# Bank order of the P·V runs, engine of the weight-scale operations, and room for side work in a fused attention and GLU kernel

## The chip, the cores and the metric

The kernel runs on one core of a Trainium2 chip. The metric is the device time of one execution in microseconds (us). Three executions of the kernel before took 2601.76, 2604.6 and 2605.78 us; their median is 2604.6 us. The five engines of a core, with the short names that the profile uses, are TensorE (PE, its weight loads PEld), VectorE (DVE), ScalarE (ACT), GpSimd (POOL) and SyncE (SP, which only issues transfers).

## The reference

The input `x` has 2048 rows of 576 numbers. Everything is computed in float32:

```python
xn = layernorm(x)                         # over the 576 columns
qkv = xn @ wqkv                           # 32 heads of 18 columns each
p = softmax(q @ k.T * 18 ** -0.5)         # 2048 x 2048 for each head
s = (p @ v, heads side by side) @ wo
h = gelu(xn @ w_gate) * (xn @ w_up)       # 2048 x 4608, tanh form of gelu
g = silu(h @ w_down)
out = x + s * g
```

## The kernel before

**Precision.** Most products are taken in float16 with each float32 operand split in a high and a low half (`XHT`, `XL` for the normalized input, `whi`, `wlo` for weights, `hhi`, `hlo` for the hidden values), three products for one. To split a weight block, its largest magnitude is found, and the block is scaled by a power of two.

**Preparing a weight block.** `prep` makes a list of small steps ("pieces") for each block: load by DMA, seven maxima on VectorE (`amax`, `amaxd`, lines 248 and 253), a trip through DRAM that spreads the maximum over the partitions (`par`, `spread`), then on VectorE `top` (line 295), `power` (line 300: the bits of the exponent are kept), `floor` (line 306), `inverse` (a reciprocal, line 311, and a multiplication, line 312), then the splits (`split_hi` on ScalarE, line 330, and `split_lo` mostly on GpSimd, lines 337 and 338), and for the 18 gate/up/down blocks `units` and `back` (lines 316 to 324), which give the factors by which results are scaled back. From `power` on these are eight small operations, each on 128 partitions by one or two numbers. Where a block is `urgent` (the first two) some of this goes another way. There are 25 such blocks: the first attention block, V, four more attention blocks, 18 gate/up/down blocks and the output projection.

**The order of work is written out by the program.** Each engine executes its instructions in the order in which they are issued here. The main loop goes over 16 pairs of heads, `p`, with 64 steps `i` each; `now` is 64 `p` + `i`. A step issues the scores for the softmax (`qk2`, line 1337, into the PSUM bank `s2`, then the exponential on ScalarE, line 1343), the scores for the row maxima of a later pair (`qk1`, line 1285, into `s1`, then the maximum on VectorE, line 1288), and beside these one share of the other products: slots of a gate/up product or a projection (`Pair`, line 468, called "g" in the code), a stage of a down product (`DownPair`, line 728, bank `md`), or a run of P times V.

**Gate/up pairs.** A `Pair` writes two PSUM banks, `ma` (gate) and `mb` (up). When its last slot is issued, `end` puts an evacuation of the gate bank on ScalarE at once (line 633); one step later the up bank follows (line 644), and one more step later four elementwise operations on GpSimd (`cubic`, lines 656 to 659). Later come a tanh on ScalarE (line 662), two operations on GpSimd (669, 670), and the split of the result (684, 691).

**Runs of P times V.** The exponentials wait in `pend`, two half steps to a unit. When a `Pair` has closed (`gs.closed`), the next step issues a run: `flush` takes the units out of `pend` in bursts, each burst into the next bank of the tuple that it is given, and cuts a burst where one block of queries ends (the unit whose third entry is `NT - 1`) and the next begins. `burst` (line 1362) adds its bank to `osum` on VectorE (line 1370) or, for the first burst of a query block, copies it (line 1368). With a down stage in the same step the banks are `ma`, `mb`; without one they are `md`, `ma`. The `Pair` that comes after the run begins with `ma`.

**Side work.** `subtick(room, most)` is called once a step. It first gives out deferred operations that are due (`Deferred.advance`), then at most `most` pieces of the weight preparation, first in, first out. `room` says how many microseconds of ScalarE ("A") and VectorE ("V") work may be given out; a piece with the cost `None` always fits. A `Rest` holds the list until so much planned time has gone by, a `Gate` until a condition holds. In the step of a run `room["V"]` is 2.2, or 1.4 if a down product ends in it (`late`); in other steps it is 0.75 or 0.25.

Of the kernel before, what the change touches and what calls it, by code (L numbers as in the profile page):

```python
# [12 lines left out]
F32 = mybir.dt.float32  # L13
F16 = mybir.dt.float16
I32 = mybir.dt.int32
# [5 lines left out]
P = 128  # L21
# [64 lines left out]
def on_dve(t=0.7):  # L86
    return {"V": t}
# [7 lines left out]
def kernel(ctx: ExitStack, tc: tile.TileContext, x, wqkv, wo, w_gate, w_up, w_down, out):  # L95
# [55 lines left out]
    def subtick(room=FREE, most=3):  # L151
        defer.advance(room)
        n = 0
        while bg and n < most:
            if isinstance(bg[0], Gate):
                if not bg[0].open():
                    return
                bg.popleft()
                continue
            if isinstance(bg[0], Rest):  # L160
                if not bg[0].over():
                    return
                bg.popleft()
                continue
            cost, fn = bg[0]
            if not defer.fits(cost):
                return
            defer.spend(cost)
            bg.popleft()
            n += 1  # L170
            if fn is None:
                return
            fn()
# [36 lines left out]
    def prep(name, parts, n, down=None, urgent=False, free=None, dfree=None, lead=1, vec=()):  # L210
# [80 lines left out]
        def top():  # L291
            k = w.k
            if not urgent:
                w.mg = sm.tile([P, 2], F32, tag="mg", name=f"mg_{name}")
                nc.vector.tensor_reduce(w.mg[:, 0:k], w.mb.rearrange("p a k -> p k a"), op=ALU.max, axis=AX.X)

        def power():
            k = w.k
            w.E = sm.tile([P, 2], F32, tag="E", name=f"E_{name}", bufs=4)
            nc.vector.tensor_scalar(  # L300
                w.E[:, 0:k].bitcast(I32), w.mg[:, 0:k].bitcast(I32), 0x7F800000, None, op0=ALU.bitwise_and
            )

        def floor():
            k = w.k
            nc.vector.tensor_scalar(w.E[:, 0:k], w.E[:, 0:k], 2.0 ** -60, None, op0=ALU.max)

        def inverse():
            k = w.k
            w.s = sm.tile([P, 2], F32, tag="s", name=f"s_{name}")  # L310
            nc.vector.reciprocal(w.s[:, 0:k], w.E[:, 0:k])
            nc.vector.tensor_scalar(w.s[:, 0:k], w.s[:, 0:k], 2.0 ** 14, None, op0=ALU.mult)

        def units():
            w.uE = sm.tile([P, 2], F32, tag="uE", name=f"uE_{name}", bufs=4)
            nc.vector.tensor_scalar(w.uE[:, 0:1], w.E[:, 0:1], 2.0 ** -24, None, op0=ALU.mult)
            nc.vector.tensor_scalar(w.uE[:, 1:2], w.s[:, 0:1], 2.0 ** -44, None, op0=ALU.mult)

        def back():
            w.c = sm.tile([P, 1], F32, tag="c", name=f"c_{name}", bufs=4)  # L320
            nc.vector.tensor_scalar(
                w.c, w.E[:, 0:1], w.E[:, 0:1], 2.0 ** -9, op0=ALU.mult, op1=ALU.mult
            )
            nc.vector.tensor_tensor(w.c, w.c, w.E[:, 1:2], op=ALU.mult)

        def split_hi(t):
            if t == 0:
# [30 lines left out]
        def add(fn, cost=None):  # L358
            pieces.append((cost, fn))

        def rest(span):
            if not urgent:
                pieces.append(Rest(span))
# [16 lines left out]
        rest(6.5)  # L380
        add(top, on_dve(0.4))
        for fn in (power, floor, inverse):
            add(fn, on_dve(0.2))
        rest(0.5)
        if free is not None:
            pieces.append(Gate(free))
        for t in range(5):
# [2 lines left out]
                add(lambda t=t: split_lo(t - 1), low_cost[t - 1])  # L390
        add(lambda: split_lo(4), low_cost[4])
        if down is not None:
            add(units, on_dve(0.2))
            add(back, on_dve(0.3))
            add(fin)
            pieces.append(Gate(dfree))
            add(lambda: dsplit_hi(0), act)
            add(lambda: dsplit_hi(1), act)
            add(lambda: dsplit_lo(0), on_pool(3.0))
            add(lambda: dsplit_lo(1), on_pool(3.0))  # L400
            add(dfin)
        else:
            add(fin)
# [1058 lines left out]
    k = 0  # L1462
# [113 lines left out]
    def flush(tags):  # L1576

        for tag in tags:
            if not pend:
                return  # L1580
            n = next((k + 1 for k, u in enumerate(pend) if u[2] == NT - 1), len(pend))
            burst(pend[:n], tag)
            del pend[:n]
# [36 lines left out]
    for p in range(NPAIR):  # L1620
# [3 lines left out]
        for i in range(4 * NT):  # L1624
# [64 lines left out]
            else:  # L1689
# [16 lines left out]
                if gs.closed:  # L1706
                    gs.closed = False
                    if late:
                        dn.evac()
                        dn = None  # L1710
                    subtick({"A": 2.2, "V": 1.4 if late else 2.2, "T": 0.7 + 0.86 * len(pend) + 0.73 * d}, 6)
                    flush(("ma", "mb") if d else ("md", "ma"))
                    summed = not d
                else:
                    quick = late or step is not None and step[2] < 1.45 and len(bg) < 70
                    subtick({
                        "A": 0.75, "V": 0.25 if quick else 0.75,
                        "T": 2.0 if step is None else 0.45 + step[2],
                    })
                    if late:  # L1720
                        dn.evac()
                        dn = None
                    g_run(7 if step is None else step[1] or 0)
                    if behind:
                        dn = DownPair()
                        dn.run()
# [73 lines left out]
```

## Time and profile before

| | |
|---|---|
| runs | 2601.76, 2604.6, 2605.78 us |
| profiled execution, its own time | 2606.5 us |
| its span, first to last instruction | 2604.7 us |
| mean granted TensorE clock | 0.995 |
| busy: VectorE | 1929.3 us (74%) |
| busy: ScalarE | 1660.6 us (64%) |
| busy: GpSimd | 1508.9 us (58%) |
| mean DMA traffic | 46 GB/s |

The first exponential of the main loop starts at 214.7 us; before it the input is normalized, V and the first heads are projected, and the first gate/up products begin. The profile's views that matter here are the page, the waits (who waited for whom, how long in total, how often, the longest), the timeline (start, duration, engine, line, what is written and read; in brackets the idle time of the engine before it and what ended it), and the groups of instructions by line. The rows themselves stand where the prediction uses them.

### The profile page before, as it was taken

What the parts mean: (1) busy time and instruction counts of PE and PEld (TensorE: products, weight loads), DVE (VectorE), ACT (ScalarE), POOL (GpSimd) and SP (SyncE); (2) the same over time, 40 slices, a digit from 0 to 9 for tenths busy, and PEclk for the clock granted to TensorE, in tenths of its full rate; (3) what the DMA queues carried; (4) which work ended last, traced back from release to release, by engine and by line L of the source; (5) the groups of instructions that cost most, each with busy time, mean ns of one, the idle gap of its engine ahead of it and who ended that gap; (6) DMA issues with size and microseconds to landing.
All of it is one profiled execution on the core that took longest, in us unless ns stands there. A gap on an engine that the chain in (4) does not pass through costs nothing.

```text
span 2604.7 us, 60777 instructions
## 1 busy us (share of the span) xinstructions
PE 2510.1 (96%) x25800; PEld 1326.4 (51%) x25800; DVE 1929.3 (74%) x2712; ACT 1660.6 (64%) x2081; POOL 1508.9 (58%) x1428
## 2 busy tenths in 40 slices
PE   6899999999999999999999999999999999999988
PEld 6564545455544545455554454555445444454555
DVE  7587778777877778777777777777777777677644
ACT  5225666666767666766666666767666665766664
POOL 4246663576537543757667575748566675757513
PEclk9999999999999999999999999999999999999999
DMA  4431021201130112111010110101111111010124
GB/s 143 124 107 24 12 58 57 60 18 44 39 84 19 27 37 64 39 30 51 14 50 13 38 45 21 49 15 38 29 33 29 37 29 40 17 38 8 41 62 137
DMA packets 134300, 118.68 MB, mean 46 GB/s; under 512 B 60176, under 2 KB 113064, under 8 KB 134028
## 3 DMA queue, kind: packets, MB, share of 16 engines
q1 hardware_dynamic: 128892, 105.23, 15.1%
q0 software_dynamic: 2432, 6.54, 0.8%
q8 instruction: 201, 3.29, 0.6%
q10 hardware_dynamic: 2704, 3.03, 0.4%
q14 instruction: 71, 0.58, 0.1%
HBM read 84.89 MB, written 29.61 MB: 44 GB/s over the span
## 4 chain that ended last, share of the span: by engine, by line
PE 81%; DVE 9%; ACT 4%; issue 2%; DMA 2%; POOL 2%; SPq 0%; ACTq 0%; DVEq 0%; POOLq 0%
PE mb_t L468 16%; PE ma_t L468 15%; PE md_t L728 15%; PE md_t L1362 9%; PE s L1337 8%; PE s L1285 8%; PE ma_t L1362 6%; DVE PM L1288 3%; ACT P L1343 1%; PE md_t L907 1%; DVE osb L1370 1%; DVE m_c L248 1%; PE mb_t L1362 1%; DMA QT<-QD 1%; PE mb_t L907 1%
## 5 line engine op out<-in xcount | busy, mean ns | idle before, releaser
L1288 DVE TENSOR_REDUCE PM<-s 128x2 f32<-128x1024 f32 x1024 | 1250.5, 1223 | 340.9 <-PE s L1285 332.6
L1343 ACT ACTIVATE P<-s,etab 128x1024 f32<-128x1024 f32 x896 | 995.7, 1112 | 615.7 <-PE s L1337 600.1
L468 PE MATMUL ma_t<-XHT,whi_c 64*128 64x512 f16 x1440 | 542.5, 377 | 10.5 <-DVE osb L1368 5.6
L468 PE MATMUL mb_t<-XHT,whi_c 64*128 64x512 f16 x1440 | 542.5, 377 | 3.8 <-DVE touch L436 2.0
L468 PE MATMUL ma_t<-XHT,wlo_c 64*128 64x512 f16 x1296 | 487.9, 376 | 0.0
L468 PE MATMUL mb_t<-XHT,wlo_c 64*128 64x512 f16 x1152 | 433.5, 376 | 0.0
L468 PE MATMUL ma_t<-XL,whi_c 64*128 64x512 f16 x1152 | 433.3, 376 | 0.0
L468 PE MATMUL mb_t<-XL,whi_c 64*128 64x512 f16 x1152 | 433.2, 376 | 0.0
L1285 PE MATMUL s<-KT,QT 54*128 54x512 f16 x2048 | 399.5, 378 | 20.8 <-DVE PM L1288 9.5
L1337 PE MATMUL s<-QT,KT 56*128 56x512 f16 x2048 | 406.2, 380 | 5.3 <-ACT P L1343 1.6
L468 PEld LDWEIGHTS <-whi_c 64*128 64x128 f16 x5184 | 276.7, 94 | 245.0 <-issue 29.5
L728 PE MATMUL md_t<-dhi_c,hhi 64*128 64x288 f16 x2304 | 341.8, 283 | 7.3 <-DVE osb L1370 2.3
L728 PE MATMUL md_t<-dhi_c,hlo 64*128 64x288 f16 x2304 | 341.5, 282 | 0.0
L728 PE MATMUL md_t<-dlo_c,hhi 64*128 64x288 f16 x2304 | 340.9, 282 | 0.0
L669 POOL TENSOR_SCALAR tw<-tw 128x512 f32<-128x512 f32 x144 | 90.9, 632 | 408.1 <-ACT tw L662 408.0
L728 PEld LDWEIGHTS <-hhi 64*128 64x128 f16 x4608 | 247.2, 94 | 141.3 <-issue 22.8
L1362 PE MATMUL md_t<-P,VT 128*32 128x512 f32 x2480 | 293.0, 596 | 0.7 <-ACT P L1343 0.5
L691 POOL TENSOR_TENSOR hlo<-gv,hhi 128x512 f16<-128x512 f32 x144 | 168.0, 1167 | 206.4 <-ACT hhi L684 195.8
L1337 PEld LDWEIGHTS <-KT 56*128 56x128 f16 x2048 | 126.0, 94 | 244.4 <-issue 158.0
L656 POOL TENSOR_TENSOR tw<-gs 128x512 f32<-128x512 f32 x144 | 150.6, 1046 | 138.8 <-ACT gs L633 138.3
L748 DVE SCALAR_TENSOR_TENSOR y<-md_t,c_c,y 128x576 f32<-128x576 f32 x272 | 219.0, 805 | 8.3 <-PE md_t L728 8.2
L468 PEld LDWEIGHTS <-wlo_c 64*128 64x128 f16 x2592 | 139.6, 94 | 121.8 <-issue 1.1
(253 smaller groups left out, 4070.3 us busy)
## 6 DMA issues: line engine op xcount, KB each, us to landing
draw_c<-in_B_w_down SPq DMA_DIRECT2D x18, 576.0 KB
raw_c<-in_B_w_gate SPq DMA_DIRECT2D x18, 512.0 KB
raw_c<-in_B_w_up SPq DMA_DIRECT2D x18, 512.0 KB
obr<-rd SPq DMA_DIRECT2D x30, 256.0 KB
KT<-KD SPq DMA_DIRECT2D x32, 224.0 KB
QT<-QD SPq DMA_DIRECT2D x32, 216.0 KB
VS<-vst POOLq DMA_DIRECT2D x16, 304.0 KB, 4.0
VT<-VS SPq DMA_DIRECT2D x16, 304.0 KB
```

What stands on the lines that cost most here:

```text
L468: nc.tensor.matmul(o, lw, xx, start=self.stage == 0 and self.k == 0, stop=self.stage == 1 and self.k == self.slots - 1, skip_group_check=True,
L656: gp.tensor_tensor(st["t"], st["g"], st["g"], op=ALU.mult)
L669: gp.tensor_scalar(st["t"], st["t"], 1.0, 1.0, op0=ALU.mult, op1=ALU.add)
L691: gp.tensor_tensor(hs.lo[:, ft], st["v"], hs.hi[:, ft], op=ALU.subtract)
L728: nc.tensor.matmul(self.t.t[:, hf, 0:288], a[r, ft, sl], b[r, ft, 288 * hf:288 * hf + 288], start=self.stage == 0 and k == 0, stop=self.st ...
L748: nc.vector.scalar_tensor_tensor(yy, y, w.c, yy, op0=ALU.mult, op1=ALU.add)
L907: nc.tensor.matmul(o, a, b, start=self.stage == 0 and self.k == 0, stop=self.stage == 1 and self.k == len(terms) - 1, skip_group_check=True,)
L1285: nc.tensor.matmul(s1[:, h], QT[p][r, P * qt:P * qt + P], KT[p][r, 512 * kb:512 * kb + 512], start=True, stop=True)
L1288: nc.vector.tensor_reduce(PM[p][:, :, qt, kb:kb + 1], s1, op=ALU.max, axis=AX.X)
L1337: nc.tensor.matmul(s2[:, h], KT[p][r, P * kt:P * kt + P], QT[p][r, 512 * qb:512 * qb + 512], start=True, stop=True)
L1343: nc.scalar.activation(pt, s2, AF.Exp, scale=ETAB[j0])
L1362: nc.tensor.matmul(t.t[qd:qd + 32, :], VT[p][:, c0:c0 + 32], pt[:, h], start=kt == k0, stop=kt == k1, skip_group_check=True,)
```

## The change

Three things are edited.

1. `flush` is given `("ma", "md")` instead of `("md", "ma")` where no down stage runs in the step and a query block ends inside the run, before its last unit (`two`).
2. For blocks that are not urgent, `floor`, `inverse`, `units` and `back` are issued to GpSimd (`small_ops`). `power` stays on VectorE and gets a second operation that makes the complement of the exponent in `w.s`; `inverse` is then one operation (minimum and multiplication) instead of a reciprocal and a multiplication. `back` becomes three operations instead of two. `floor` and `inverse` of these blocks, and `units` and `back` always, have no cost for the planner now. The pause after them is 1.0 instead of 0.5.
3. In the step of a run the room for VectorE is 0.8 instead of 1.4 if a down product ends in it; otherwise it stays 2.2 while `now` is under 256 (the first four pairs of heads) and is 1.5 instead of 2.2 from then on.

```diff
+        small_ops = nc.vector if urgent else nc.gpsimd
+        EXPO = 0x7F800000
+
         def power():
             k = w.k
             w.E = sm.tile([P, 2], F32, tag="E", name=f"E_{name}", bufs=4)
+            w.s = sm.tile([P, 2], F32, tag="s", name=f"s_{name}")
+            mg = w.mg[:, 0:k].bitcast(I32)
+            nc.vector.tensor_scalar(w.E[:, 0:k].bitcast(I32), mg, EXPO, None, op0=ALU.bitwise_and)
             nc.vector.tensor_scalar(
-                w.E[:, 0:k].bitcast(I32), w.mg[:, 0:k].bitcast(I32), 0x7F800000, None, op0=ALU.bitwise_and
+                w.s[:, 0:k].bitcast(I32), mg, EXPO, EXPO, op0=ALU.bitwise_and, op1=ALU.bitwise_xor
             )
 
         def floor():
             k = w.k
-            nc.vector.tensor_scalar(w.E[:, 0:k], w.E[:, 0:k], 2.0 ** -60, None, op0=ALU.max)
+            small_ops.tensor_scalar(w.E[:, 0:k], w.E[:, 0:k], 2.0 ** -60, None, op0=ALU.max)
 
         def inverse():
             k = w.k
-            w.s = sm.tile([P, 2], F32, tag="s", name=f"s_{name}")
-            nc.vector.reciprocal(w.s[:, 0:k], w.E[:, 0:k])
-            nc.vector.tensor_scalar(w.s[:, 0:k], w.s[:, 0:k], 2.0 ** 14, None, op0=ALU.mult)
+            small_ops.tensor_scalar(
+                w.s[:, 0:k], w.s[:, 0:k], 2.0 ** 61, 2.0 ** 13, op0=ALU.min, op1=ALU.mult
+            )
 
         def units():
             w.uE = sm.tile([P, 2], F32, tag="uE", name=f"uE_{name}", bufs=4)
-            nc.vector.tensor_scalar(w.uE[:, 0:1], w.E[:, 0:1], 2.0 ** -24, None, op0=ALU.mult)
-            nc.vector.tensor_scalar(w.uE[:, 1:2], w.s[:, 0:1], 2.0 ** -44, None, op0=ALU.mult)
+            small_ops.tensor_scalar(w.uE[:, 0:1], w.E[:, 0:1], 2.0 ** -24, None, op0=ALU.mult)
+            small_ops.tensor_scalar(w.uE[:, 1:2], w.s[:, 0:1], 2.0 ** -44, None, op0=ALU.mult)
 
         def back():
             w.c = sm.tile([P, 1], F32, tag="c", name=f"c_{name}", bufs=4)
-            nc.vector.tensor_scalar(
-                w.c, w.E[:, 0:1], w.E[:, 0:1], 2.0 ** -9, op0=ALU.mult, op1=ALU.mult
-            )
-            nc.vector.tensor_tensor(w.c, w.c, w.E[:, 1:2], op=ALU.mult)
+            small_ops.tensor_tensor(w.c, w.E[:, 0:1], w.E[:, 0:1], op=ALU.mult)
+            small_ops.tensor_scalar(w.c, w.c, 2.0 ** -9, None, op0=ALU.mult)
+            small_ops.tensor_tensor(w.c, w.c, w.E[:, 1:2], op=ALU.mult)
...
         add(top, on_dve(0.4))
         for fn in (power, floor, inverse):
-            add(fn, on_dve(0.2))
-        rest(0.5)
+            add(fn, on_dve(0.2) if urgent or fn is power else None)
+        rest(0.5 if urgent else 1.0)
...
         if down is not None:
-            add(units, on_dve(0.2))
-            add(back, on_dve(0.3))
+            add(units)
+            add(back)
             add(fin)
...
-                    subtick({"A": 2.2, "V": 1.4 if late else 2.2, "T": 0.7 + 0.86 * len(pend) + 0.73 * d}, 6)
-                    flush(("ma", "mb") if d else ("md", "ma"))
+                    subtick({"A": 2.2, "V": 0.8 if late else 2.2 if now < 256 else 1.5, "T": 0.7 + 0.86 * len(pend) + 0.73 * d}, 6)
+                    two = any(u[2] == NT - 1 for u in pend[:-1])
+                    flush(("ma", "mb") if d else ("ma", "md") if two else ("md", "ma"))
                     summed = not d
```

## The prediction

> **What bounds the kernel now.** I read the page first, then the busy times by stretch, then who waited for whom on PE in the main loop, 240 to 2400 us.
>
> ```profile
> span 2604.7 us, 60777 instructions
> PE 2510.1 (96%) x25800; PEld 1326.4 (51%) x25800; DVE 1929.3 (74%) x2712; ACT 1660.6 (64%) x2081; POOL 1508.9 (58%) x1428
> ...
> 240.00:2400.00 2160.00, 2122.59 (x21768) 1079.62 (x21762) 1655.13 (x2264) 1448.18 (x1790) 1335.07 (x1227) 1.00 0.14 36
> ...
> PE s L1285 <- DVE PM L1288: 7.9, 8, 2.1
> PE ma_t L468 <- DVE osb L1368: 5.6, 10, 2.3
> PE ma_t L468 <- DVE osb L1370: 3.9, 6, 1.1
> ```
>
> PE is the bound: 96% of the span, and in the main loop 2122.59 of 2160 us. The change removes no matmul, so its reach there is the 37.4 us in which PE idles, and most of that waits for DVE. The second line of waits is the one that the bank order aims at: ten times a gate/up pair wanted bank ma, and the copy out of it by line 1368 was not done. The other two are places where DVE came late after a run of P times V, with small side work ahead of it. The head and the tail (0 to 240, 2400 to the end) hold few of the steps that change: the two urgent blocks keep DVE and have four small operations up to the scale before and after. I cost them at nothing. A change within 0.2%, some 5.2 us, can't be told from none here; that is the meaning of "same" below.
>
> **Part A, the bank order.** One of the ten boundary runs, then a worse one, the other long one, and a run that begins with ma today because a down stage stands ahead of it:
>
> ```profile
> 1262.07 0.69 ACT L633 ACTIVATE gs<-ma_t,uE_c 128x512 f32<-128x512 f32 x1 [0.68 <-PE ma_t L468]
> 1262.33 1.07 PE L1362 MATMUL md_t<-P,VT 128*32 128x512 f32 x8
> 1262.81 0.13 PEld L1362 LDWEIGHTS ma_t<-P,VT 128*32 128x32 f32 x4 [0.32 <-ACT gs L633]
> 1263.59 0.68 DVE L1370 TENSOR_TENSOR osb<-md_t,osb 128x512 f32<-128x512 f32 x1
> 1264.32 0.69 DVE L1368 COPY osb<-ma_t 128x512 f32<-128x512 f32 x1
> 1265.07 0.37 PE L468 MATMUL ma_t<-XHT,whi_c 64*128 64x512 f16 x1 [0.27 <-DVE osb L1368]
> ...
> 746.18 0.68 DVE L1370 TENSOR_TENSOR osb<-md_t,osb 128x512 f32<-128x512 f32 x1
> 746.78 0.68 DVE L1368 COPY osb<-ma_t 128x512 f32<-128x512 f32 x1
> 747.51 0.56 PE L468 MATMUL ma_t<-XHT,whi_c 64*128 64x512 f16 x1 [2.35 <-DVE osb L1368]
> ...
> 1340.84 1.86 DVE L248 TENSOR_REDUCE m_c<-raw_c 128x1 f32<-128x512 f32 x3
> 1343.95 0.37 PE L468 MATMUL ma_t<-XHT,whi_c 64*128 64x512 f16 x1 [1.04 <-DVE osb L1368]
> ...
> 960.25 1.07 PE L1362 MATMUL ma_t<-P,VT 128*32 128x512 f32 x8 [0.48 <-ACT gs L633]
> ```
>
> What goes: eight of the ten waits are the plain kind, 0.27 us each (5.6 less 2.35 and 1.04, by eight). With ma first, its sum runs on DVE while PE works on the burst in md, so ma is free in time, and eight times 0.27 go, 2.2 us. At 747 us DVE itself was late (three maxima ahead); PE would be let go at the end of the sum instead of the end of the copy, 0.60 us earlier. At 1344 us one maximum fewer stands ahead (part C), and the whole 1.04 goes. The md copy is late next, but a down stage that follows such a run is put behind the gate/up slots by `behind`, so nobody asks for md at once.
>
> What comes: ma can't be written before ScalarE has read the gate out of it. In the first rows that evacuation runs from 1262.07 to 1262.76; the burst started at 1262.33 in md, and the weight load for ma was released at 1262.81, by the evacuation. With ma first the whole run starts at 1262.81, 0.48 us later, and PE has nothing in between. At 960 us just that wait is in the trace, 0.48 us, even with a down stage ahead of it. So each plain boundary loses 0.48 and gains 0.27: +0.21 by eight, +1.7. At 747 the burst's delay lies inside DVE's lateness, so it stays at -0.6; at 1344 it is 0.48 less 1.04, -0.6. **A: +0.5 us.** Its ends are -3.8 (the new wait is covered after all) and +4.2 (0.48 ten times less 0.6, were the DVE lateness not met again).
>
> **Part B, the small operations.** One late stretch, the worst of its kind, with the start of the gate evacuation:
>
> ```profile
> 2203.88 0.69 ACT L633 ACTIVATE gs<-ma_t,uE_c 128x512 f32<-128x512 f32 x1 [0.19 <-PE ma_t L468]
> ...
> 2207.04 1.27 POOL L658 TENSOR_TENSOR tw<-tw,gs 128x512 f32<-128x512 f32 x1
> 2207.07 1.27 DVE L306 TENSOR_SCALAR E_c<-E_c 128x2 f32<-128x2 f32 x1
> 2208.27 1.26 POOL L659 TENSOR_TENSOR gv<-gv,gs 128x512 f32<-128x512 f32 x1
> 2208.64 0.92 DVE L312 TENSOR_SCALAR s_c<-s_c 128x2 f32<-128x2 f32 x1
> 2211.33 0.39 PE L1285 MATMUL s<-KT,QT 54*128 54x512 f16 x2 [2.06 <-DVE PM L1288]
> ...
> L306 DVE TENSOR_SCALAR E_c<-E_c x18: 92/170/1282, 163.9 to 2207.1; 128x2 f32<-128x2 f32 x18
> ```
>
> `floor` works on two numbers a partition, takes 170 ns in the median and 1282 at most. At 2207 it lasts until GpSimd's operation ends (2208.34 against 2208.31), then the multiplication likewise (until 2209.56, against 2209.53). So a small DVE operation is held by a large one on GpSimd, and DVE's next work, the sum of the run and the row maximum, comes late: PE loses 2.06 us. The Trainium skill's page "SBUF — State Buffer", section "Who interferes with whom", has the rule: a DVE tensor_scalar in a two-port mode and a GpSimd operation take one pair of ports exclusively, for the whole instruction. The trace agrees (the two ends, 0.03 us apart).
>
> In the step of a run `top`, `power`, `floor`, `inverse` are all issued in the run's own subtick, while `cubic` is issued one step later. So the new GpSimd `floor` and `inverse` stand ahead of `cubic` in GpSimd's queue, and wait there for `power`: GpSimd is idle while DVE does its two bit operations, and these aren't held. Where, instead, `power` falls a step later, `cubic` is ahead, and both bit operations can be held, one after the other. PE's waits behind these chains:
>
> ```profile
> 439.91 0.39 PE L1285 MATMUL s<-KT,QT 54*128 54x512 f16 x2 [1.04 <-DVE PM L1288]
> ...
> 522.58 0.37 PE L468 MATMUL ma_t<-XHT,whi_c 64*128 64x512 f16 x1 [1.11 <-DVE osb L1370]
> ...
> 716.83 0.30 PE L728 MATMUL md_t<-dhi_c,hhi 64*128 64x288 f16 x2 [0.78 <-DVE osb L1370]
> ...
> 1503.67 1.22 DVE L300 TENSOR_SCALAR E_c<-mg_c 128x2 int32<-128x2 int32 x1
> 1504.83 1.26 POOL L659 TENSOR_TENSOR gv<-gv,gs 128x512 f32<-128x512 f32 x1
> 1505.00 0.30 PE L728 MATMUL md_t<-dhi_c,hhi 64*128 64x288 f16 x2 [1.00 <-DVE touch L436]
> ...
> 1611.08 0.37 PE L468 MATMUL ma_t<-XHT,whi_c 64*128 64x512 f16 x1 [1.01 <-DVE osb L1370]
> ```
>
> At 523, 1611 and 2211 us the chain was held in a run's step: 1.1 + 1.0 + 2.1 go. At 440 nothing was held; the reciprocal and the multiplication go, half a microsecond. At 717 it was `units` and `back` ahead of the sum: 0.8 goes. At 1505 the wait is that of a down stage in an ordinary step, so I take `power` there to be of the later kind: it stays held for 1.22, and the second bit operation comes as line 659 begins, so it is held for about another 1.2: +1.2. **B: -5.5 + 1.2 = -4.3 us.** Ends: -6.5 (at 1505 nothing is held either, and its 1.0 goes) and -2.0 (the second operation is held wherever `floor` was: 0.9 goes at 2211, the multiplication's hold, half a microsecond each at 440, 523 and 1611, 0.8 at 717, and 1505 costs its 1.2).
>
> GpSimd gets seven operations a gate/up block. The trace has no such one; by the nearest rows
>
> ```profile
> L1166 POOL TENSOR_TENSOR xn<-xt,xn 128x64 f16<-128x64 f32 x16 | 5.1, 320 | 33.2 <-ACT xn L1165 31.9 <-PE pv_t L415 1.3
> L1276 POOL MEMSET VT<- 128x16 f32 x16 | 1.8, 112 | 0.0
> ...
>   POOL tw L658: 3.0, 5
> ...
> 1165.52 1.27 POOL L658 TENSOR_TENSOR tw<-tw,gs 128x512 f32<-128x512 f32 x1
> ...
> 1170.98 0.62 ACT L662 ACTIVATE tw<-tw 128x512 f32<-128x512 f32 x1
> ```
>
> one lies between 112 ns (16 columns written) and 320 ns (64 columns read and written); I take 200, nearer to the memset because there are fewer columns still. 18 x 7 x 0.2 is 25 us of an engine that is idle for some 1100, so its time is covered. The added wait isn't free: behind `floor` in GpSimd's queue stands `cubic`, behind that the tanh on ScalarE, behind that exponentials, and PE. `cubic` can start now when the gate evacuation ends (2204.57 in the stretch above), some 2.3 us ahead of `power` (0.2 before `floor` at 2207.07), and would start about 0.8 us after `power` begins (two bit operations, `floor`, `inverse`, 0.2 each): up to 3.1 us later. The tanh in the last two rows, one case, begins 4.2 us after the GpSimd result that it needs, and ScalarE's idle time for it is 3.0 us over five waits in all. I put down +0.4 us, between nothing and 3 us.
>
> **Part C, less room beside a run.**
>
> ```profile
> L1343 ACT ACTIVATE P<-s,etab x896: 1095/1113/1127, 214.7 to 2575.3; 128x1024 f32<-128x1024 f32 x180
> ...
> 1038.34 0.39 PE L1285 MATMUL s<-KT,QT 54*128 54x512 f16 x2 [2.12 <-DVE PM L1288]
> ...
> 2178.68 0.30 PE L728 MATMUL md_t<-dhi_c,hhi 64*128 64x288 f16 x2 [0.83 <-DVE osb L1368]
> ```
>
> Sixteen pairs of heads take from 214.7 to 2575.3, 147.5 us each, so `now` is 256 near 805 us. From there a room of 1.5 lets two pieces at 0.7 through in place of three. Three maxima of 0.62 us (the row at 1340.84, 1.86 for three) stood ahead of DVE's sum at these two places; one fewer is -0.6 each. The piece that is pushed out goes to an ordinary step, where DVE has a quarter of its time free; I found no PE wait over 0.4 us behind a lone maximum of an ordinary step, so I cost that at nothing, with 3 us as its other end (five such waits of 0.6). **C: -1.2 us.**
>
> **The sum.** +0.5 - 4.3 + 0.4 - 1.2 = -4.6 us. The profiled execution took 2606.5 us, 1.8 beyond its span, and would come to 2601.9. The median of the runs is 1.9 below the profiled one, so the forecast for a median is 2604.6 - 4.6 = **2600.0 us**, 0.18% faster.
>
> **The rivals.** *Faster.* All small operations pass unheld, B at -6.5 with A and C as they are: 2604.6 + 0.5 - 6.5 - 1.2 = 2597.4; if the gate evacuation is covered as well (A at -3.8), 2593.1. For it: the hold needs GpSimd at work, and its queue now stops at `floor`. Against: the rows at 1262 and 960 us show the evacuation as the later of the two. *Nothing gained.* By the skill's rule the first to issue keeps the ports; should `cubic` mostly be ahead, the second bit operation takes the place of `floor`, B is -2.0, and the sum +0.5 - 2.0 + 0.4 - 1.2 = -2.3: 2602.3. For it: 1503.67. Against: the run began long before it there, and `cubic` is issued a step after the run's subtick. *Slower.* GpSimd, stopped at `floor` until a late DVE reaches `power`, passes its lateness to tanh, exponentials and PE. It decides from the point where `cubic` comes more than 4.2 us later than now; at 1 us beyond that in each of 18 blocks it costs 18 us less the 4.6: 2618. Against it: the 3.1 us above.
>
> **How the numbers follow.** The forecast's case has 0.50, with an own range of 2597 to 2604; its part under 2599.4 (0.2% faster) is about 0.14, the rest "same". Faster rival 0.28. Nothing gained 0.14, same. Slower rival 0.08. So faster 0.42, same 0.50, slower 0.08. The range, 2593.5 to 2605.5, takes in the faster rival but its outer end and the case of nothing gained, and leaves out the slower one.
>
> **What would show it.** Copies by line 1368 read md instead of ma at some ten places; PE's wait for them at ma is gone, and a new wait, ma at line 1362 for the gate evacuation, has about 4 us in ten waits where 1.8 in two stood. Lines 306, 312 and 316 to 324 stand on POOL; the bit operations at line 300 and the next take 170 ns, except where they meet `cubic`. The waits of line 1285 for line 1288 fall from 7.9 to some 4. Waits of the tanh for line 658 of over 6 us in all would speak for the slower rival; no new wait at line 1362 would show part A wrong, and a PE total below 2509 or above 2512 would show that the matmuls themselves changed.

## The result and the profile after

The changed kernel takes 2589.04 us (median of six runs, 2588.17 to 2589.88) against 2604.98 us before (2601.76 to 2606.47). The ratio is 0.994, with a 95% interval from 0.9929 to 0.9951: 16 us or 0.6% faster, clear of noise, beyond the low end of the forecast's range (2593.5) and more than three times the 4.6 us that were forecast. The page of the changed kernel (its span, then busy time and share of each engine):

```profile
span 2588.1 us, 60831 instructions
PE 2503.7 (97%) x25800; PEld 1317.9 (51%) x25800; DVE 1898.9 (73%) x2594; ACT 1661.0 (64%) x2081; POOL 1537.7 (59%) x1564
```

Read this beside the page of before. The matmuls are the same 25800, VectorE does 118 operations fewer, GpSimd 136 more. The span is 16.6 us shorter, but PE's busy time, which no step of the prediction touched, fell by 6.4 us of that. The waits of PE between 240 and 2400 us (who, on whom, us in total, times, longest):

```profile
PE ma_t L1367 <- ACT gs L638: 4.7, 10, 1.0
PE s L1290 <- DVE PM L1293: 4.6, 7, 1.5
PE s L1342 <- ACT P L1348: 4.0, 5, 1.6
PE ma_t L473 <- DVE osb L1375: 2.6, 5, 1.0
```

The first line is new in this size (1.8 in two waits before): runs that begin with ma wait for the gate evacuation. The waits for line 1368 (now 1373) at ma are gone, 5.6 us before. The row maxima fell from 7.9 to 4.6. The third line is new too: two waits of 1.6 us for exponentials.

Both kernels issue the same matmuls in the same order, apart from bank names and 14 of the 25800 that change places with a neighbour. So their starts can be matched one by one, and every change of the distance between two starts belongs to one place. Those that the argument uses, worked out from the two traces:

```
matmul at (before, after), us   change there   what it waited for before / after
 439.91   438.51    -0.60   row maximum, behind the small operations / the same, shorter
 522.58   519.31    -1.28   sum, behind held small operations / nothing
 523.18   519.32    -0.59   the copy after it / nothing
 716.83   711.84    -0.99   sum, behind units and back / nothing
 741.84   737.82    +0.97   nothing / evacuation of ma (bank order)
 747.51   741.93    -1.57   copy out of ma / sum out of ma (bank order)
1038.34  1029.84    -0.66   row maximum, three maxima ahead / the same, shorter
1262.33  1254.60    +0.47   nothing / gate evacuation (bank order; seven more like it)
1265.07  1256.90    -0.43   copy out of ma / nothing     (bank order; seven more like it)
1343.95  1334.49    -1.20   copy out of ma, three maxima ahead / nothing
1505.00  1494.43    -1.16   down stage, behind a held power / nothing
1547.04  1538.23    +1.78   nothing / exponential
1551.96  1542.37    -0.79   sum of a run / the same, shorter
1611.08  1600.10    -1.17   sum, behind held small operations / nothing
1866.48  1853.55    -0.79   down stage, behind a held floor / nothing
1906.05  1894.93    +1.79   nothing / exponential
2178.68  2165.81    -1.00   copy, three maxima ahead / nothing
2211.33  2195.81    -2.22   row maximum, behind held small operations / nothing
```

Two things are to be seen. A plain boundary wait shows 0.27 us idle in the brackets, but costs 0.43 from start to start: the idle time counts only from the modelled end of the last matmul, which lasts 0.38 us where the next could start after 0.21. Some 0.16 us of each wait therefore stands under "busy". And some waits go on costing after they end. The timeline of the kernel before, PE's rows around the worst boundary wait (start, duration):

```profile
747.51 0.56 PE L468 MATMUL ma_t<-XHT,whi_c 64*128 64x512 f16 x1 [2.35 <-DVE osb L1368]
...
747.87 0.63 PE L468 MATMUL ma_t<-XL,whi_c 64*128 64x512 f16 x1
...
748.29 0.63 PE L468 MATMUL ma_t<-XHT,wlo_c 64*128 64x512 f16 x1
```

and its windows view over that stretch and the next (length, PE busy and matmuls, granted clock, DMA share, GB/s):

```profile
747.50:751.10 3.60, 3.59 (x18) 0.53 0.27 78
751.10:754.70 3.60, 3.59 (x34) 1.00 0.13 36
```

The matmuls run in pairs, one for ma and one for mb (left out here). After the wait, the pairs start 0.42 us apart instead of 0.21, and a matmul lasts 0.63 instead of 0.38. The granted clock is 0.53 for 3.6 us, and 18 matmuls pass in place of 34: some 1.7 us beyond the wait. The same follows the wait at 2211 us. Both are gone in the changed kernel's profiled run. The two stretches at half speed make up some 3.1 us of the 6.4 us that PE's "busy" time lost. The rest lies in the hidden parts of waits and in small steps, which were not counted one by one.

### The profile page after: what moved, and what is told of

Read it like the earlier page. It is cut to its first block, busy times and chain, and to the rows that moved or that the text cites. A ratio compares the mean times of both kernels' runs of the same rounds, so it can differ in the third digit from the quotient of the medians.

```text
span 2588.1 us, 60831 instructions
## 1 busy us (share of the span) xinstructions
PE 2503.7 (97%) x25800; PEld 1317.9 (51%) x25800; DVE 1898.9 (73%) x2594; ACT 1661.0 (64%) x2081; POOL 1537.7 (59%) x1564
## 4 chain that ended last, share of the span: by engine, by line
PE 83%; DVE 6%; ACT 4%; POOL 3%; issue 2%; DMA 1%; ACTq 0%; SPq 0%; DVEq 0%; POOLq 0%
PE mb_t L473 16%; PE ma_t L473 15%; PE md_t L733 15%; PE md_t L1367 10%; PE s L1342 8%; PE s L1290 8%; PE ma_t L1367 6%; DVE PM L1293 2%; ACT P L1348 1%; PE md_t L912 1%; DVE osb L1375 1%; PE mb_t L1367 1%; PE mc_t L492 1%; PE mb_t L912 1%; PE pv_t L492 1%
```

## The experiments

Each kernel was timed against the kernel before on the same chip, in five rounds. That kernel's medians there were 2604.25 to 2605.73 us, so a difference of 1 to 2 us between two rows of the table shows nothing by itself.

| kernel | median, us | ratio to before, 95% interval |
|---|---|---|
| changed kernel | 2589.04 | 0.9940 (0.9929 to 0.9951) |
| `a_banks`: bank order alone | 2603.75 | 0.9996 (0.9987 to 1.0005) |
| `b_small`: small operations alone | 2596.97 | 0.9972 (0.9962 to 0.9983) |
| `c_room`: smaller room alone | 2597.36 | 0.9972 (0.9963 to 0.9981) |
| `a_and_b` | 2596.14 | 0.9967 (0.9954 to 0.9979) |
| `b_and_c` | 2590.45 | 0.9950 (0.9936 to 0.9964) |
| `columns` | 2596.41 | 0.9969 (0.9958 to 0.9981) |
| `columns_room` | 2596.83 | 0.9971 (0.9961 to 0.9982) |
| `units_room` | 2599.26 | 0.9982 (0.9973 to 0.9990) |
| `units_dve` | 2589.27 | 0.9941 (0.9928 to 0.9955) |
| `units_early` | 2588.17 | 0.9941 (0.9929 to 0.9954) |
| `halves` | 2602.72 | 0.9994 (0.9985 to 1.0003) |
| `columns_room_halves` | 2607.09 | 1.0009 (1.0000 to 1.0018) |
| `shift_a` | 2615.22 | 1.0039 (1.0027 to 1.0052) |
| `shift_b` | 2618.31 | 1.0055 (1.0041 to 1.0069) |
| `c_room_clear` | 2601.28 | 0.9989 (0.9981 to 0.9998) |
| `c_room_behind` | 2601.86 | 0.9984 (0.9975 to 0.9993) |

### The three parts, alone and in pairs

`a_banks` is the kernel before with this edit:

```diff
+                    two = any(u[2] == NT - 1 for u in pend[:-1])
-                    flush(("ma", "mb") if d else ("md", "ma"))
+                    flush(("ma", "mb") if d else ("ma", "md") if two else ("md", "ma"))
```

> The kernel before with the bank order of boundary runs alone. Theory: each of the eight plain boundaries trades a stall of 0.43 us (start to start) at the next gate/up pair for one of 0.47 us at the run's first burst, and only the two boundaries at 747 and 1344 us gain, 0.6 us each: about -1 us, 2603 to 2604.5, PE waits at ma for the gate evacuation in about ten places. Rival: the new wait is mostly covered, the old ten waits go: -4 us or more.

It gave -1.0 us (2604.71 to 2603.75), within noise. The matched starts show the trade: eight times +0.40 to +0.48 at the run's first burst and -0.43 at the next pair, -0.60 net at 747 us and at 1344 us. In the changed kernel, the boundary that the prediction showed at 1262 us reads (timeline, start and duration):

```profile
1253.86 0.69 ACT L638 ACTIVATE gs<-ma_t,uE_c 128x512 f32<-128x512 f32 x1 [0.68 <-PE ma_t L473]
...
1254.60 1.07 PE L1367 MATMUL ma_t<-P,VT 128*32 128x512 f32 x8 [0.40 <-ACT gs L638]
...
1255.73 0.69 DVE L1375 TENSOR_TENSOR osb<-ma_t,osb 128x512 f32<-128x512 f32 x1 [0.27 <-PE ma_t L1367]
...
1256.59 0.69 DVE L1373 COPY osb<-md_t 128x512 f32<-128x512 f32 x1 [0.17 <-PE md_t L1367]
...
1256.90 0.38 PE L473 MATMUL ma_t<-XHT,whi_c 64*128 64x512 f16 x1
```

The run now starts when ScalarE has emptied ma (1254.55), and the pair behind it starts without a wait, while the copy out of md still runs. One wait took the other's place.

`b_small` is the changed kernel with the old `flush` and the old room.

> The kernel before with the small operations of the weights' scales on GpSimd alone (bit operations on VectorE, pause 1.0), bank order and room as before. Theory: this is the bulk of the change. PE's steps of 0.6 to 3.4 us at 440, 523, 717, 1505, 1611, 1866 and 2211 us go, some 11 us, and two new waits of 1.6 us for exponentials, which stand behind the five operations of units and back in GpSimd's queue, come: -7 to -9 us, 2595 to 2598. Rival: the gain is the smaller room's, and this part alone gives -2 us or less.

It gave -7.7 us, as the theory had it, but not by all of the theory's terms (see the waits for exponentials below). Its two bit operations (durations in ns, least, median, most):

```profile
L305 DVE TENSOR_SCALAR E_c<-mg_c x18: 169/170/1220, 164.1 to 2200.4; 128x2 int32<-128x2 int32 x18
...
L306 DVE TENSOR_SCALAR s_c<-mg_c x18: 155/162/165, 164.2 to 2200.5; 128x2 int32<-128x2 int32 x18
```

The first is held once, by 1.05 us, where `cubic` was ahead of it; the second, issued right behind, is never held. In the kernel before, `floor` took up to 1282.

`c_room` is the kernel before with the new room alone:

```diff
-                    subtick({"A": 2.2, "V": 1.4 if late else 2.2, "T": ...
+                    subtick({"A": 2.2, "V": 0.8 if late else 2.2 if now < 256 else 1.5, "T": ...
```

> The kernel before with less room for VectorE beside the runs alone. Theory: the waits at 1038, 1344 and 2178 us shrink by 0.6 to 1 us each: -2 to -3 us, 2602 to 2603. Rival: it is this room that keeps the chains of small operations away from the runs, and it gives -6 us or more alone; third: pieces pushed into ordinary steps cost as much there, 0.

-7.4 us, against the theory and for its first rival. By the matched starts it removes not only 0.7 at 1038, 0.6 at 1344 and 1.4 at 2178 us, but also the waits at 1505, 1611, 1866 and 2211 us, whose chains had nothing to do with maxima: with fewer pieces given out beside the runs, the list of pieces is at another point when those steps come, and the chains fall elsewhere. Against that it pays 6.2 us at 665 us, of which more below.

The pairs `a_and_b` and `b_and_c` leave one part out of the changed kernel.

> The changed kernel without the smaller room (bank order and small operations only). If the parts add up: 2604.6 - 1.0 - 7.7 = 2596. If the smaller room's gain alone (7.4) was the same stalls as the small operations', so that something else pays in the changed kernel: under 2593.

> The changed kernel without the bank order (small operations and smaller room only). Theory: the bank order trades 0.43 us for 0.47 at eight places and gains only where VectorE was late, 0.6 to 0.8 us at 740 us, and nothing more at 1331 since fewer maxima stand there: 2589 to 2591. Rival: it is worth 3 us or more in the changed kernel: 2592 or more.

2596.14 and 2590.45: both as the theory had it. The three parts alone add up to -1.0 - 7.7 - 7.4 = -16.1, the whole change gave -15.9. Inside the changed kernel the bank order is worth some 1.4 us, which isn't clear of noise (the two profiled executions have the same span, 2588.1 us), and the smaller room some 7.

That the parts add up is in part luck. `b_small` and `c_room` each remove the waits at 1611, 1866 and 2211 us, which can go only once. `c_room` pays 6.2 us at 665 us that the changed kernel doesn't pay, and the changed kernel pays 3.6 us in waits for exponentials that neither part pays alone.

### Is it the hold by GpSimd?

`columns` moves nothing to GpSimd. It only cuts three VectorE operations of a chain into one for each column:

```diff
-            nc.vector.tensor_scalar(w.E[:, 0:k], w.E[:, 0:k], 2.0 ** -60, None, op0=ALU.max)
+            for c in range(k):
+                nc.vector.tensor_scalar(w.E[:, c:c + 1], w.E[:, c:c + 1], 2.0 ** -60, None, op0=ALU.max)
...
```

> The kernel before, all small operations left on VectorE, but power, floor and the multiplication of inverse are issued for one column at a time (two operations of one number a partition in place of one of two). Theory of the hold by GpSimd's running operation: operations on one column are not held, all take under 220 ns, and though VectorE gets three more operations a block the time falls by 2 to 6 us. Rival (what counts is how many operations stand ahead of the run's sum): no gain, or up to 2 us slower, and single durations of over 1 us stay.

It gave -8.3 us, as much as moving the operations and more than the 2 to 6 us of the theory. More operations stood ahead of the sums, so their number isn't what counted. `power` and `floor` of `columns`, where the gate/up blocks' 36 one-column operations stand (ns, least, median, most):

```profile
L301 DVE TENSOR_SCALAR E_c<-mg_c x36: 143/150/155, 163.7 to 2202.5; 128x1 int32<-128x1 int32 x36
...
L308 DVE TENSOR_SCALAR E_c<-E_c x36: 96/145/154, 163.9 to 2202.7; 128x1 f32<-128x1 f32 x36
```

Not one is held, in the same places beside `cubic`: at 2202.64 us `floor` starts together with `cubic`'s third operation and takes 153 ns, where the prediction's row at 2207.07 us has 1.27 us. The Trainium skill's page "SBUF — State Buffer", section "Who interferes with whom", ties the hold to two-port modes of tensor_scalar; that dividing a two-number operation avoids it is what these rows show.

### The new waits for exponentials

In the changed kernel, before the wait at 1538 us, GpSimd and ScalarE (timeline):

```profile
1533.26 0.22 POOL L322 TENSOR_SCALAR uE_c<-E_c 128x1 f32<-128x1 f32 x1
...
1534.40 0.19 POOL L329 TENSOR_TENSOR c_c<-c_c,E_c 128x1 f32<-128x1 f32 x1
...
1534.55 0.62 POOL L674 TENSOR_SCALAR tw<-tw 128x512 f32<-128x512 f32 x1
1535.25 1.27 POOL L675 TENSOR_TENSOR gv<-gv,tw 128x512 f32<-128x512 f32 x1
...
1536.55 0.63 ACT L689 ACTIVATE hhi<-gv 128x512 f16<-128x512 f32 x1 [1.99 <-POOL gv L675]
...
1537.08 1.10 ACT L1348 ACTIVATE P<-s,etab 128x1024 f32<-128x1024 f32 x1
...
1538.23 0.39 PE L1342 MATMUL s<-QT,KT 56*128 56x512 f16 x2 [1.61 <-ACT P L1348]
```

The five operations of `units` and `back` take 1.3 us of GpSimd between the last weight split and the second half of the gelu; ScalarE stands for 2 us in front of `hhi`, the exponential behind it is late, and PE waits. So lateness on GpSimd does reach PE, as the slower rival had it, at two places and by other operations than the ones that it named. But moving the operations isn't enough for it. PE's waits for these exponentials between 240 and 2400 us in `b_small`, then in `b_and_c`:

```profile
PE s L1342 <- ACT P L1348: 0.9, 3, 0.4
...
PE s L1342 <- ACT P L1348: 4.1, 5, 1.7
```

`a_and_b` hasn't got the long waits either (1.1 us in four, the longest 0.4). In `b_small` the same five operations stand ahead of `cubic` (from 1533.49 us; `cubic` starts at 1534.77), and no such wait follows. With the smaller room they fall between the weight split and the gelu. Three kernels tried to take this away: a GpSimd cost for the two pieces (`units_room`), the two left on VectorE (`units_dve`), and the two issued with `inverse` and empty pieces in their place (`units_early`):

```diff
-            add(units)
-            add(back)
+            add(units, on_pool(0.6))     # units_room
+            add(back, on_pool(0.9))
...
+            add(units, on_dve(0.2))      # units_dve, with the old units() and back()
+            add(back, on_dve(0.3))
...
+            if down is not None:         # units_early, at the end of inverse()
+                units()
+                back()
```

> The changed kernel, with units and back given a GpSimd cost (0.6 and 0.9 us), so that the planner issues them only when little GpSimd work is outstanding. Theory: the two waits for exponentials at 1538 and 1895 us, 1.8 us each, come from these five operations standing between the last weight split and the second half of the gelu; they go: -3 to -4 us against the changed kernel, about 2585.5. Rival: those waits come from the second half of the gelu being late anyway, no change; or the blocks get ready later and PE waits in the first 600 us, slower.

> The changed kernel, with units and back left on VectorE as before (floor and inverse stay on GpSimd). Theory: the same two waits go (-3.6 us), and at one or two places about 1 us comes back on VectorE, as at 717 us of the kernel before: 2585 to 2588. Rival: VectorE was the reason for the gain of the small operations, and this part of it is worth more than 3 us: 2590 or more.

> The changed kernel, with units and back issued to GpSimd together with inverse, ahead of the weight splits, and empty pieces where they stood, so that the planner's order of all else stays. Theory: the two waits of 1.6 us for exponentials at 1538 and 1895 us go, 3.6 us; the first half of the gelu comes 1.4 us later, which the tanh mostly hides: 2585 to 2587. Rival: the delay at the tanh takes it back: 2589 or more.

`units_dve` and `units_early` cut the two waits from 1.6 to 0.37 us each (their matched starts: twice -1.25), which shows the cause. The time didn't follow: 2589.27 and 2588.17 can't be told from the changed kernel, and both lie above what was expected (2585 to 2588, and 2585 to 2587). `units_dve` paid 0.99 at 717 us and 0.49 at 510 us back. `units_early` has the fastest median, within the intervals. `units_room` went the way of its second rival, 10 us slower than the changed kernel: with the later pieces came a wait of 3.1 us for a row maximum at 480 us and one of 3.5 at 667 us, both with half-speed matmuls behind them.

### Both bursts in one bank

`halves` gives a boundary run without a down stage one md tile and puts its two bursts in the two halves:

```diff
-                    flush(("ma", "mb") if d else ("ma", "md") if two else ("md", "ma"))
+                    flush(("ma", "mb") if d else "halves" if two else ("md", "ma"))
```

> The changed kernel, but a boundary run without a down stage puts both its bursts into the two halves of the md bank and never touches ma. Theory: both the wait for the gate evacuation (0.47 us, ten places) and the older wait for the copy are gone: -4 to -5 us against the changed kernel, 2584 to 2585, no wait at line 1367 for the gate evacuation at those ten. Rival: the next down stage then waits for md, and the time comes back: 2588 to 2590.

A miss, for a reason that none of the expectations had: 13.7 us slower than the changed kernel. The halves are one tile, and its second burst waits until the first half has been summed (timeline of `halves`):

```profile
1263.49 0.68 DVE L1375 TENSOR_TENSOR osb<-md_t,osb 128x512 f32<-128x512 f32 x1
...
1264.23 1.06 PE L1367 MATMUL md_t<-P,VT 128*32 128x512 f32 x8 [0.92 <-DVE osb L1375]
```

1 to 3 us at each of ten places. Two separate tiles of one bank each were not tried.

> The kernel before with one-column small operations on VectorE (nothing moved to GpSimd), the smaller room beside the runs, and both bursts of a boundary run in the halves of md. Theory: the hold by GpSimd was the whole gain of moving the operations, so this gives what the changed kernel gives, less its new waits (10 x 0.47 and 2 x 1.8 us): 2580 to 2585. Rival: VectorE has some 25 us more work than in the changed kernel, and that costs: 2589 or more.

2607.09: `columns_room`, below, with the same 10 us on top. It says nothing on VectorE's extra work.

### The smaller room, or the place of the chains?

`shift_a` lengthens the pause before `top` from 6.5 to 9, `shift_b` the one after the load from 13 to 18; `columns_room` is `columns` with the smaller room.

> The kernel before with the pause before the chain of small operations lengthened from 6.5 to 9 us of planned time, nothing else; room, engines and banks as before. Theory (place): the chains that are held fall into other steps, so the long waits at 523, 1505, 1611, 1866 and 2211 us change singly, some go and some come, and the time moves by up to 6 us either way, without less room. Rival (the room itself is what counts): same time within 2 us, 2603 to 2607.

> The kernel before with the pause after a weight block's load lengthened from 13 to 18 us of planned time, nothing else, so that the maxima and all that follows fall some two steps later. Theory (place): like the other shift, a move of up to 6 us either way. Rival (the room itself is what counts): 2603 to 2607.

> The kernel before with one-column small operations on VectorE and the smaller room beside the runs. If the smaller room acted by keeping held chains out of the runs' steps, nothing is held here and it adds only what three maxima ahead of a sum cost: -1 to -3 us beyond one-column operations alone (2596.4), 2593.5 to 2595.5. If it acts in its own right, by fewer operations ahead of the sums at many places, it adds its -7 us: about 2589.

The shifts cost 10.8 and 13.9 us, beyond even the theory's range, though the waits at 1611, 1866 and 2211 us were gone or short in both (the one at 1505 in `shift_a`). So where a chain falls does matter, but a shift also moves other work. In `shift_b` it came too late for the first blocks (waits of PE between 170 and 480 us):

```profile
PE ma_t L468 <- POOL wlo_c L338: 12.9, 7, 2.3
```

`columns_room` came out at 2596.83, neither expectation: +0.4 beside `columns`. Its matched starts say why the room seems worth nothing there: some 6 us of gains, and one loss of 6.2 us at 665 us (3.5 in a wait, 2.7 in half-speed matmuls behind it). `c_room`, `shift_a`, `shift_b`, `units_room` and `columns_room_halves` wait there too, the kernel before, the changed one, `b_small` and `columns` don't. It is the transfer of the row maxima through DRAM, which runs at the end of each pair of heads. `c_room`, SyncE's queue and ScalarE's (timeline; q marks the issuing of a transfer):

```profile
651.00 0.41 SPq L229 DMA_DIRECT2D raw_c<-in_B_w_gate  x1
...
653.31 3.39 SPq L241 DMA_DIRECT2D draw_c<-in_B_w_down  x1
...
656.79 0.48 ACTq L1311 DMA_DIRECT2D md<-rms  x1
656.80 0.64 SPq L1277 DMA_DIRECT2D VT<-VS  x1
...
662.07 0.54 ACTq L1315 DMA_DIRECT2D QT<-md  x2
...
665.66 0.75 PE L1337 MATMUL s<-QT,KT 56*128 56x512 f16 x2 [3.33 <-DMA QT<-md]
```

and the kernel before:

```profile
643.40 0.40 SPq L229 DMA_DIRECT2D raw_c<-in_B_w_gate  x1
...
649.36 0.65 SPq L1277 DMA_DIRECT2D VT<-VS  x1
...
658.91 0.46 ACTq L1311 DMA_DIRECT2D md<-rms  x1
661.21 0.54 ACTq L1315 DMA_DIRECT2D QT<-md  x2
```

The second transfer is issued when the first has landed: 2.3 us before, 5.3 in `c_room`, where a weight block's 1.6 MB were issued 3.5 to 5.8 us ahead of it instead of 13.2 to 15.5. Two kernels were to take that collision out of `c_room`: `c_room_clear` gives out no load in steps 54 to 62, `c_room_behind` issues this one load on ScalarE's queue behind the two transfers.

```diff
+            pieces.append(Gate(lambda: not 54 <= pos[0] <= 62))   # c_room_clear, before load
...
+        q = nc.scalar if name == "c4" else nc.sync                # c_room_behind, with
+            pieces.append(Gate(lambda: pos[0] == 63))             # this before c4's load
```

> The kernel with the smaller room alone, and weight loads kept out of the steps 54 to 62 of each pair of heads, where the row maxima go through DRAM. Theory (collision): the wait at 665 us for the maxima, 3.3 us, and the half-speed matmuls behind it, together 6.2 us, go: 2590 to 2594. Rival: they are of no account, or the later load costs as much elsewhere: 2596 or more.

> The smaller room alone, with the one weight load that lands at 651 us issued from ScalarE's queue behind the two transfers of the row maxima. Theory (collision): the transfer that took 5.3 us takes 2.3 again, the wait at 665 us (3.3 us) and the half-speed matmuls behind it go, 6.2 us less some 1 to 3 us for five issues on ScalarE and the later block: 2592 to 2594.5. Rival: the collision isn't that load's doing, or it costs nothing net: 2597 or more.

Both missed in time. In `c_room_clear` the load was issued at 652.7 us all the same: SyncE had stood there for 11.8 us until the last weight split of an earlier block (line 339), so the gate didn't set the load's time. In `c_room_behind` the collision did go: the first transfer took 2.3 us again (659.37 to 661.68), and the matched starts show -3.51 there. But ScalarE stood behind its own five issues (timeline):

```profile
669.23 0.69 ACT L1348 ACTIVATE P<-s,etab 128x512 f32<-128x512 f32 x1 [4.76 <-DMA raw_c<-in_B_w_up]
...
670.54 0.61 PE L1340 MATMUL s<-QT,KT 56*128 56x512 f16 x2 [3.59 <-ACT P L1349]
```

and gave it back; both kernels are some 4 us slower than `c_room` itself. So the collision's part in the wait is shown; that `c_room` would gain its full 6 us without it is not. Nor is it shown which transfer is the partner. The load of V (`VT`, 304 KB), next in SyncE's queue, was issued in `c_room` 0.01 us after the first transfer of the row maxima, and in `c_room_behind` it had gone out at 641.58 us, so it left together with the weight block.

## Why the prediction was wrong

Of the 11 us that the forecast missed, some 6 lie in part C, 4 in part B with its queue term and 1.5 in part A, by the parts alone.

**What bounds the kernel.** PE is the bound and the matmuls are unchanged, as stated. The step that failed here is the pricing of waits by PE's idle time ("37.4 us in which PE idles"), with a PE busy total that moves by at most a microsecond or two unless "the matmuls themselves changed". The total fell by 6.4 us with the same matmuls. Each wait hides some 0.16 us in "busy", and a wait of 2 us or more can be followed by 3.4 us at half clock. Both were in the trace of before.

**Part A** was forecast at +0.5 and came out at -1.0 alone and about -1.4 in the changed kernel, inside its ends and neither clear of noise. The mechanism was right: the gate evacuation is the later of the two, and the new wait stands at all the places. The mis-sized term is the old wait, 0.43 us for the bracket's 0.27, so that a plain boundary comes to +0.04 instead of +0.21.

**Part B** was forecast at -4.3 and gave -7.7 (by its interval -4.4 to -9.9). The hold by GpSimd is shown twice over, by `columns` and by the rows of `b_small`. Two steps failed. The first is the +1.2 at 1505 us, for a second bit operation held in its turn: `power` was held there as forecast (1220 ns), the second never was, 165 ns at most. The second is the missing after-effects: in the profiled execution 2211 us cost 2.2 and about 1.4 at half speed, not 2.1. The queue order was right (no bit operation beside a run was held). The +0.4 for GpSimd's queue was put at the wrong place: not `cubic` behind `floor`, but the second half of the gelu behind `units` and `back`, which cost 3.6 us, and only together with part C. Those five operations were priced (25 us of idle GpSimd) and never placed in the queue.

**Part C** was forecast at -1.2 and gave -7.4 alone, -7.1 in the changed kernel. This is the main error. The step that failed is that the forecast counted the two places where three maxima stood ahead of a sum, took all else to stay where it was, and cost the pushed-out pieces at nothing. A smaller room also delays the whole list of pieces, and other chains and loads leave, or reach, the runs. From `a_and_b` to the changed kernel the main loop of the profiled runs is 6.4 us shorter. Steps of over 0.5 us make only 1.5 of it, 6.2 of gains less 4.8 of losses (3.6 of them the exponentials). The other 4.9 come in smaller steps, which no list of long waits holds; 1.2 of these is the half-speed stretch behind the wait at 1032 us in `a_and_b`. What stays open is how much of the 7 us is less work ahead of the sums and how much is a lucky place: the two shifts of mere place went the other way by 11 and 14 us.

**The rivals.** The faster one had the right sign, and was 8 us short for the same reasons. The one that gains nothing was refuted by the second bit operation's 165 ns. The slower one's sign stayed away: the tanh waited 2.3 us for `cubic` in all, not over 6.

## What to carry to other kernels

Match the two instruction lists of a reordered kernel and read costs from start to start; the idle time before an instruction leaves out a part of each wait, and says nothing of the half-speed work that may follow it. A planner's budget is never a local edit: whatever it delays lands elsewhere, so bound such a part by a shift of the same list, not by the stalls that it is meant for. A small VectorE operation of two numbers beside a busy GpSimd can take seven times its length; cutting it into single columns was as good as moving it (2596.4 and 2597.0 us), and leaves GpSimd's queue alone. With the smaller room on top it was not (2596.8 against 2590.5), since that list of pieces met the transfers at 665 us.

## What the runs showed of the hardware

The clock fell after short waits, and not after each. Of the 29 waits of PE of 2.0 to 3.6 us in the main loop of these 18 kernels, each profiled once, 17 were followed by matmuls at half speed, for 3.4 or 6.8 us. The wait of 2.35 us at about 745 us was followed by it in the kernel before and in `columns`, not in `b_small` and `b_and_c`.

It goes with where the wait falls. In every trace the half-speed stretches from 100 us on begin whole multiples of 3.413 us apart (747.56, 2211.88 and 2529.32 us in the kernel before: 429 and 93 of them). Cut into pieces on that grid, the main loops of all the kernels have 14 pieces in which PE was idle for 1.98 us or more, and all 14 were followed by one at half speed. Of 40 with 1.45 to 1.97 us idle it was 7, and below that none, unless the clock was down already. In the kernel before, the wait lies whole in the piece from 744.15 to 747.56 us (PE busy for 1.06 us), and the clock granted in the next is 0.50. In `b_small` the piece from 741.83 to 745.24 us holds only a part of the same wait (PE busy for 1.71), and the next has 1.00.

The Trainium skill's page "TensorE: Matmul & The Clock Gate", Part 1, describes a free-running window of 3413 ns whose activity sets the clock, with half rate after an idle window. The grid agrees with it; that a wait of 2.06 us, shorter than a window, is enough, the rows at 2211 us show against the plain reading. A fall of 3.4 us cost 1.2 to 1.7 us where the starts were matched, one of 6.8 us 2.7.

GpSimd takes 190 to 250 ns for an operation on one or two numbers a partition (252 in the median for `inverse`), and they follow each other every 0.28 us, so five of them cost 1.3 us of its queue.
